# Deferring two groups' output projection until all weights are decoded, with one matmul type and a new issue order

## The chip, the cores and the metric

One core of a Trainium2 chip runs the whole program. The metric is the device time of one execution in microseconds (us), lower is better.

## The reference

Attention over 4 batches, 8 heads, 768 positions and 64 channels per head. Each query sees the keys within 15 positions of its own, and 24 block keys (the maximum over each block of 32 keys) whose values are block means; the softmax runs over both sets. The result, laid out as 3072 tokens of 512 values, goes through a gated feed-forward layer:

```python
rms = sqrt(mean(x * x) + 1e-6);  xn = x / rms * rms_g
g   = xn @ w_gate                    # 512 x 1536
h   = g * sigmoid(g) * (xn @ w_val)  # 512 x 1536
out = h @ w_out                      # 1536 x 512
```

The three weight matrices arrive as float64, two 32-bit words per value.

## The kernel before

**Units and groups.** The 3072 tokens are 24 units of 128. Units 0 to 5 (batch 0) have attention steps of their own in float32, `su_...`; units 6 to 23 have `load_unit`, `prep_k`, `scores`, `expo`, `attend`. `norm_a` and `norm_b` turn a unit's result into `xT`, the transposed f16 pair (high and low part) that the feed-forward layer reads. The feed-forward work goes by nine groups of 384, 128, 256 and then six times 384 tokens (`GROUPS`). The width 1536 of the hidden layer is 12 blocks f of 128.

**Feed-forward steps.** `gate_val g f T` makes two products of 12 f16 matmuls each into two PSUM banks (tile `gv`), then on ScalarE a tanh, on VectorE two multiplications, and splits the gated value `th` into a pair (`hh`, `hl`). `project g f` multiplies the pair with block f of w_out: for each 128 tokens a triple of 128x512 matmuls (hh with both parts of w_out, hl with one), summed over all f in a bank `acc`. Groups 5 to 8 make half or all of their gated values in another way (`make_s`, `make_t`, `seven`, `swish`); the change does not touch their arithmetic.

**Weights.** `load_gv n` (n from 0 to 11; even gate, odd value) and `load_o f` (f = 0, 2, ... 10) fetch 1 MB each. `decode` turns float64 into float32: one ScalarE and two VectorE instructions of 128x1024. `decode_gv` adds a ScalarE square; `split_gv` has nine small matmuls for a norm, a scale, one ScalarE and one VectorE instruction that leave the f16 pair in `w_gv`. `decode_o` leaves w_out first as a pair of float32r tiles (a ScalarE cast, a VectorE subtraction). Groups 0, 1 and 2 (`grp < HALF`) are projected with these float32r pairs, block by block while weights still arrive. Later `scale_h`, `row_o` (squares of w_out's rows) and `scale_o` give scales, and `conv_o` turns each float32r pair into an f16 pair: two GpSimd additions, two ScalarE and two VectorE instructions of 128x512 per pair of blocks. Groups from 3 on are projected with f16 pairs and these scales.

**Rooms.** Raw weights 0, 1 and 5 to 11 go through two buffers `raw`; 2, 3 and 4 through the rooms `wo0` to `wo2`; w_out's raw words through the room of their own block pair, `wo0` to `wo5`.

**Order.** `PLAN` is the list of steps in program order. `ORDER` then fixes, for each engine's queue separately, the exact order in which its instructions issue. Each queue is served in order, so an instruction that waits holds all that stand behind it. The DMAs that the SP queue issues follow its list as well. `WARM` puts extra matmuls into TensorE's queue in the first stage.

Of the kernel before, what the change touches and what calls it, by code (L numbers as in the profile page):

```python
# [19 lines left out]
P = 128  # L20
NEG = -1.0e30
EXPO = float(1 << 23)
HALF = 3
SEVEN = 5
RAW = 2
# [7 lines left out]
SR = 6  # L33
# [11 lines left out]
su_first; su_load 0 1; su_load 1 1; su_load 2 1; su_load 3 1; su_load 4 1; su_load 5 1; su_load 0 0;  # L45
load_gv 0 1; su_k 0; su_k 1; su_k 2; su_k 3; su_k 4; su_k 5; su_v 0; su_q 0; su_v 1; su_v 2; su_v 3; su_v 4;
su_v 5; su_load 1 0; load_gv 1 1; su_load 2 0; su_fill 0; decode_gv 0; su_scores 0 0; su_fill 2; su_q 1;
su_scores 0 1; su_vsum 0; su_q 2; su_expo 0 0; su_fill 1; su_vsum 1; su_fill 5; su_v2 0; load_gain;
su_expo 0 1; su_v2 2; su_scores 1 1; su_fill 3; su_vsum 4; prep_gain; su_scores 1 0; su_vsum 3; su_vsum 2;
load_gv 2 1; load_gv 5; su_vsum 5; split_gv 0; su_attend 0 0; su_v2 1; su_attend 0 1; su_expo 1 1; su_expo 1 0;  # L50
decode_gv 1; su_attend 1 0; su_attend 1 1; su_scores 2 0; su_fill 4; su_expo 2 0; norm_a 0; decode_gv 2;
load_gv 4 1; su_attend 2 0; load_gv 3 1; split_gv 2; split_gv 1; decode_gv 3; su_scores 2 1; load_o 0 1;
su_expo 2 1; norm_b 0; su_attend 2 1; split_gv 3; load_o 2 1; norm_a 2; decode_o 2; decode_o 0; norm_a 1;
decode_gv 4; norm_b 2; norm_b 1; su_v2 3; load_o 4 1; swap_left; gate_val 0 0 384; sum_load 1 0 0 0;
sum_load 1 0 0 1; split_gv 4; su_load 3 0; su_v2 4; sum_load 1 0 0 2; gate_val 0 1 384; decode_o 4;
decode_gv 5; su_q 3; sum_fold 1 0 0 0; split_gv 5; su_scores 3 0; sum_load 1 0 0 3; sum_fold 1 0 0 1;
project 0 0 384 0; su_expo 3 0; su_scores 3 1; su_expo 3 1; su_attend 3 0; sum_load 1 0 1 0; su_v2 5;
load_gv 6; su_attend 3 1; sum_load 1 0 1 1; decode_gv 6; norm_a 3; gate_val 0 2 384; load_gv 7; decode_gv 7;
sum_fold 1 0 0 2; load_o 6; norm_b 3; gate_val 0 3 384; sum_fold 1 0 0 3; split_gv 6; load_gv 8;
sum_fold 1 0 1 0; load_o 8; su_load 4 0; split_gv 7; load_o 10; sum_fold 1 0 1 1; sum_load 1 0 1 2;  # L60
project 0 1 384 0; sum_fold 1 0 1 2; load_gv 9; sum_load 1 0 1 3; sum_load 1 1 0 0; sum_load 1 1 0 1; su_q 4;
project 0 2 384 0; decode_o 6; su_scores 4 0; su_expo 4 0; sum_fold 1 0 1 3; sum_load 1 1 0 2; su_scores 4 1;
gate_val 0 4 384; sum_fold 1 1 0 0; project 0 3 384 0; su_expo 4 1; su_attend 4 0; sum_load 1 1 0 3;
su_load 5 0; su_attend 4 1; norm_a 4; sum_fold 1 1 0 1; sum_load 1 1 1 0; sum_scale 1 0; decode_gv 8;
project 0 4 384 0; sum_load 1 1 1 1; decode_o 8; sum_fold 1 1 0 2; decode_gv 9; gate_val 0 5 384; norm_b 4;
sum_fold 1 1 0 3; split_gv 8; project 0 5 384 0; load_gv 10; sum_fold 1 1 1 0; sum_load 1 1 1 2; su_q 5;
split_gv 9; load_ks 1; su_scores 5 0; su_expo 5 0; load_k 6; su_scores 5 1; su_expo 5 1; sum_load 1 1 1 3;
# [79 lines left out]
project 8 2 384 2688; project 8 3 384 2688; seven 8 3; swish 8 2 1; swish 8 2 0; project 8 4 384 2688;  # L147
project 8 5 384 2688; seven 8 4; swish 8 3 1; swish 8 3 0; seven 8 5; swish 8 4 1; project 8 6 384 2688;
swish 8 4 0; project 8 7 384 2688; swish 8 5 1; project 8 8 384 2688; swish 8 5 0; project 8 9 384 2688;
project 8 10 384 2688; project 8 11 384 2688  # L150
"""


# [1112 lines left out]
```

## Time and profile before

| | |
|---|---|
| median of 3 runs | 724.93 us (724.47 to 725.55) |
| span of the profiled execution, first to last instruction | 722.0 us |
| busy share of the span: TensorE / VectorE / ScalarE / GpSimd | 95% / 79% / 69% / 33% |
| mean granted TensorE clock, share of full speed | 0.990 |

The profile has one execution and its span; the timed runs also hold what lies before the first and after the last instruction, 724.9 - 722.0 = 2.9 us. PE is TensorE's matmuls, PEld its weight loads, DVE VectorE, ACT ScalarE, POOL GpSimd, SP the queue that issues most DMAs. A row that names line L378 or L373 or L375 is that of a helper (subtraction, cast, copy).

### The profile page before, as it was taken

The page shows a single profiled execution, that of the slowest core. Times are in us where ns is not written, and L with a number is a line of the kernel's source. Part 1 is how long each engine was busy: PE and PEld are TensorE (multiplying, and loading weights), DVE is VectorE, ACT ScalarE, POOL GpSimd, SP SyncE. Part 2 cuts the span into 40 slices and gives each one's busy share as a digit, 9 for nine tenths or more (in the row PEclk, how much of TensorE's full clock was granted, in tenths as well). Part 3 has the DMA queues.
Part 4 walks back from the last instruction along what each step waited for, and adds up shares of the span by engine and source line. Part 5 has one row for each costly group of instructions (what it writes and reads, how often), then busy time and mean ns, then how long its engine had stood idle before and what let it go on. Part 6 is the DMA issues. An engine that isn't in the chain of part 4 may idle for free.

```text
span 722.0 us, 16185 instructions
## 1 busy us (share of the span) xinstructions
PE 683.7 (95%) x5846; PEld 496.5 (69%) x5846; DVE 573.3 (79%) x1611; ACT 501.3 (69%) x1095; POOL 241.9 (33%) x333
## 2 busy tenths in 40 slices
PE   7985999998999999999999999998999999999997
PEld 4674677766777866565555555775888787878884
DVE  4599988889779887768999979999768976766443
ACT  2588676878678875677687868868769777744433
POOL 6451221634434644633143343623124302310000
PEclk9997999999999999999999999999999999999999
DMA  9988624545897786959458696586356543321001
GB/s 195 310 294 270 207 82 119 113 105 113 132 166 153 141 140 156 180 120 179 111 103 162 143 187 139 103 148 119 85 101 116 103 113 65 67 39 44 2 1 44
DMA packets 243861, 93.34 MB, mean 129 GB/s; under 512 B 227716, under 2 KB 227716, under 8 KB 243780
## 3 DMA queue, kind: packets, MB, share of 16 engines
q1 hardware_dynamic: 239172, 84.78, 55.6%
q10 hardware_dynamic: 3456, 6.29, 2.5%
q0 software_dynamic: 1152, 1.22, 0.9%
q8 instruction: 46, 0.75, 0.4%
q14 instruction: 35, 0.29, 0.1%
HBM read 50.45 MB, written 6.59 MB: 79 GB/s over the span
## 4 chain that ended last, share of the span: by engine, by line
PE 49%; DVE 16%; ACT 14%; DMA 10%; issue 6%; SPq 3%; POOL 2%; ACTq 0%; DVEq 0%; POOLq 0%
PE acc L1215 14%; PE gv L1185 14%; PE gv L1121 13%; ACT sm L799 3%; DMA eT<-ee 2%; PE att L956 2%; DMA hn<-in_v_dram 2%; DVE sm L788 1%; PE att L825 1%; DMA hn<-in_k_dram 1%; PE att L784 1%; DVE w L482 1%; SPq L695 1%; ACT junk L1015 1%; DMA qT<-qs 1%
## 5 line engine op out<-in xcount | busy, mean ns | idle before, releaser
L1185 PE MATMUL gv<-xT,w_gv 128*128 128x384 f16 (+2 forms) x1584 | 229.5, 298 | 7.8 <-DVE th L1190 5.2
L1185 PEld LDWEIGHTS <-w_gv 128*128 128x128 f16 x1584 | 141.0, 98 | 86.5 <-issue 19.0
L1215 PE MATMUL acc<-wo,hh 128*128 128x512 f16 (+1 forms) x576 | 178.7, 392 | 0.1
L378 POOL TENSOR_TENSOR ee<-sm,ee 128x256 f16<-128x256 f32 (+1 forms) x72 | 70.5, 995 | 132.6 <-ACT ee L373 107.1
L1215 PE MATMUL acc<-wo,hl 128*128 128x512 f16 (+1 forms) x288 | 110.8, 385 | 1.6 <-DVE hl L1173 1.5
L1121 PEld LDWEIGHTS <-w_gv 128*128 128x128 f16 x1008 | 84.2, 98 | 6.0 <-issue 1.5
L799 ACT ACTIVATE sm<-sm,mx,c 128x192 f32<-128x192 f32 x144 | 70.6, 538 | 2.8
L1215 PEld LDWEIGHTS <-hh 128*128 128x128 f16 x432 | 40.4, 98 | 31.2 <-ACT hh L373 0.5
L788 DVE CUSTOM_DVE_ANT_0 sm<-att,mask 128x192 f32<-128x192 f32 x144 | 45.6, 349 | 6.3 <-PE att L784 4.3
L1121 PEld LDWEIGHTS <-wo 128*128 128x128 f16 x540 | 44.8, 98 | 6.5 <-issue 4.0
L1121 PE MATMUL gv<-S,w_gv 128*128 128x192 f16 x504 | 48.4, 246 | 0.4 <-ACT R L1148 0.2
L1121 PE MATMUL gv<-xT,w_gv 128*128 128x192 f16 x504 | 47.0, 246 | 0.1
L373 ACT CAST hh<-th 128x384 f16<-128x384 f32 (+3 forms) x66 | 29.5, 446 | 23.7 <-DVE th L1192 12.3
L766 POOL DMA_DIRECT2D v2h<-v2h x36 | 19.7, 548 | 66.8 <-ACT v2h L765 62.0
L1189 ACT ACTIVATE th<-gv,gains 128x384 f32<-128x384 f32 (+2 forms) x66 | 33.9, 513 | 11.8 <-PE gv L1185 10.2
L1215 PEld LDWEIGHTS <-hl 128*128 128x128 f16 x216 | 21.1, 98 | 30.2 <-DVE hl L1173 3.9
L378 DVE TENSOR_TENSOR hl<-th,hh 128x384 f16<-128x384 f32 (+3 forms) x66 | 36.9, 563 | 6.1 <-ACT hh L373 5.8
L1170 DVE SCALAR_TENSOR_TENSOR att<-att,R 128x384 f32<-128x384 f32 x42 | 23.2, 562 | 21.1 <-ACT att L1169 20.8
L1190 DVE SCALAR_TENSOR_TENSOR th<-th,gv 128x384 f32<-128x384 f32 (+2 forms) x66 | 31.2, 473 | 10.0 <-ACT th L1189 9.7
L626 ACT ACTIVATE junk<-hn 96x512 uint8<-96x512 f32 x48 | 30.0, 625 | 12.3 <-DMA hn<-in_v_dram 8.9
L373 ACT CAST ee<-sm 128x256 f16<-128x256 f32 (+1 forms) x72 | 34.7, 507 | 2.2 <-DMA eT<-ee 1.6
L1121 PE MATMUL gv<-xT,wo 128*128 128x192 f16 x360 | 34.9, 246 | 1.2 <-ACT xT L1108 0.6
(276 smaller groups left out, 1485.7 us busy)
## 6 DMA issues: line engine op xcount, KB each, us to landing
wo<-in_moe_w_out_dram SPq DMA_DIRECT2D x6, 1024.0 KB
out_dram<-ob ACTq DMA_DIRECT2D x23, 256.0 KB
raw<-in_moe_w_val_dram SPq DMA_DIRECT2D x5, 1024.0 KB
hn<-in_k_dram SPq DMA_DIRECT2D x24, 192.0 KB
hn<-in_v_dram SPq DMA_DIRECT2D x24, 192.0 KB
qr_l<-in_q_dram SPq DMA_DIRECT2D x17, 256.0 KB
vr_l<-in_v_dram SPq DMA_DIRECT2D x17, 256.0 KB
raw<-in_moe_w_gate_dram SPq DMA_DIRECT2D x4, 1024.0 KB
```

The source lines that it names most:

```text
L373: nc.scalar.copy(o, i)
L378: (nc.vector if ENG.get(op, "p") == "v" else nc.gpsimd).tensor_tensor(o, a, b, op=ALU.subtract)
L626: nc.scalar.activation(junk[0:96], y[:, o:o + DM], AF.Square, accum_out=d["ss"][:, j:j + 1])
L766: {"s": nc.sync, "a": nc.scalar, "p": nc.gpsimd}[ENG.get("v2q", "a")].dma_start(v2h[other, r], v2h[rs, r])
L788: nc.vector.tensor_tensor_reduce(sm[:, i, :], pt[:, j * SC:(j + 1) * SC], mask, 1.0, NEG, op0=ALU.add, op1=ALU.max, accum_out=mx[:, i:i + 1])
L799: nc.scalar.activation(sm[:, i, :], sm[:, i, :], AF.Exp, scale=s["c"][:, 0:1], bias=mx[:, i:i + 1])
L1121: nc.tensor.matmul(bank[:, i * T2:(i + 1) * T2], lhsT=right(n, wi, c), rhs=left(xi, c), start=start, stop=(i == 1 and c == 1 and wi == 1), ...
L1170: nc.vector.scalar_tensor_tensor(th, th, 1.0, g, op0=ALU.add, op1=ALU.mult)
L1185: nc.tensor.matmul(pt[:, 0:T], lhsT=w_gv[:, f - f % 2 + i, wi, c, f % 2, :], rhs=x[:, xi, c, 0:T], start=(n == 0), stop=(n == 3 * NC - 1))
L1189: nc.scalar.activation(th[:, 0:T], pg[:, 0:T], AF.Tanh, scale=f_sc[:, f - f % 2:f - f % 2 + 1])
L1190: nc.vector.scalar_tensor_tensor(th[:, 0:T], th[:, 0:T], 1.0, pg[:, 0:T], op0=ALU.add, op1=ALU.mult)
L1215: nc.tensor.matmul(accs[grp][j], lhsT=h[:, js], rhs=wo_hl[f // 2][:, wi, f % 2, :], start=(f == first and n == 0), stop=(f == (first - 1) ...
```

## The change

Group 2 is projected with f16 pairs from the start (`HALF` is gone; `KEEP = 2`). Groups 0 and 1 are gated as before, but their gated values stay in float32 in SBUF (`kept`, tiles `h0` and `h1`); when w_out has been scaled, `halve` makes the f16 pair just before each `project`. No float32r pair of w_out exists any more: `decode_o` writes float32 words in place, `conv_o` scales from them without the GpSimd additions. Raw gate and value weights take turns in the six `wo` rooms (`ROOMS`), and w_out is loaded behind them, so load n + 6 waits for decode n. The output copies of groups 0 to 2 go from VectorE to ScalarE. Some buffers of units 2 to 7 lie elsewhere (`kr_e`, `vv`, `h1`, `hhl`), and `set_v` fills the constant columns of `vv` after batch 0 instead of at the start. `PLAN` has all gate and value decodes ahead of w_out's, group 0's gates without projections between them, then group 1's, and then `project 0 ...` and `project 1 ...`; `ORDER` is new for every queue. `WARM` is unchanged.

```diff
-HALF = 3
+KEEP = 2
+ROOMS = (0, 1, 2, 3, 5, 4)
...
         def load_gv(n):
             f, i = n - n % 2, n % 2
-            shape = [P, NC, 4 * P]
-            raw = wo_room(n - 2, shape, U32) if 2 <= n < 5 else pools["early"].tile(shape, U32, name="raw", bufs=RAW)
+            raw = wo_room(ROOMS[n % 6], [P, NC, 4 * P], U32)
...
         def decode_o(f):
-            w = decode(raws.pop(("o", f)))
-            wo_hl[f // 2] = wo_room(f // 2, [P, 2, 2, DM], F32R)
-            hi, lo = (wo_hl[f // 2][:, j].rearrange("p f d -> p (f d)") for j in range(2))
-            copy("wo", hi, w)
-            sub("wolo", lo, w, hi.bitcast(F32))
+            decode(raws.pop(("o", f)), wo_raw[f // 2][:, 0:2 * DM])
...
         def conv_o(i):
-            w = wo_hl[i]
-            t = []
-            for a in range(2):
-                x = pools["late"].tile([P, DM], F32, name="cv", bufs=4)
-                nc.gpsimd.tensor_tensor(x, w[:, 0, a].bitcast(F32), w[:, 1, a].bitcast(F32), op=ALU.add)
-                t.append(x)
...
+            w = wo_raw[i][:, 0:2 * DM].bitcast(F32).rearrange("p (a x) -> p a x", a=2)
+            n = wo_hl[i] = wo_raw[i][:, 2 * DM:4 * DM].bitcast(F16).rearrange("p (j a x) -> p j a x", j=2, a=2)
             for a in range(2):
                 sc = hs_t["o_sc"][:, 2 * i + a:2 * i + a + 1]
-                nc.scalar.activation(n[:, 0, a], t[a], AF.Copy, scale=sc)
+                nc.scalar.activation(n[:, 0, a], w[:, a], AF.Copy, scale=sc)
...
         def gate_val(grp, f, T):
+            if grp < KEEP:
+                if grp not in kept:
+                    kept[grp] = pools["early"].tile([P, NF, T], F32, name=f"h{grp}")
+                th = kept[grp][:, f]
             else:
-                hh = mp.tile([P, 384], F32R, name="hh")
-                hl = mp.tile([P, 384], F32R, name="hl")
+                th = mp.tile([P, 384], F32, name="th")[:, 0:T]
...
+            if grp >= KEEP:
+                hh, hl = hs[grp, f] = half_pair()[1:]
+                copy("hh", hh[:, 0:T], th)
+                sub("hl", hl[:, 0:T], th, hh[:, 0:T])
+
+        def halve(grp, f, T):
+            hh, hl = hs[grp, f] = half_pair()[1:]
+            th, sc = kept[grp][:, f], hs_t["h_sc"][:, 0, f:f + 1]
+            nc.scalar.activation(hh[:, 0:T], th, AF.Copy, scale=sc)
+            nc.vector.scalar_tensor_tensor(hl[:, 0:T], th, sc, hh[:, 0:T], op0=ALU.mult, op1=ALU.subtract)
...
         def project(grp, f, T, tok0):
+            if grp < KEEP:
+                halve(grp, f, T)
...
-                    if grp < HALF:
-                        copy("ob", ob, accs[grp][j].rearrange("p (h d) -> p h d", h=H))
-                    else:
-                        nc.scalar.activation(ob, accs[grp][j].rearrange("p (h d) -> p h d", h=H), AF.Copy, scale=hs_t["o_iv"])
+                    nc.scalar.activation(ob, accs[grp][j].rearrange("p (h d) -> p h d", h=H), AF.Copy, scale=hs_t["o_iv"])
```

## Rows read from the trace of the kernel before

**Rows 1.** Busy time per stretch: PE, PEld, DVE, ACT, POOL, granted clock, DMA share, GB/s

```profile
40.00:80.00 40.00, 30.00 (x221) 22.71 (x221) 38.47 (x88) 31.86 (x48) 13.70 (x20) 0.87 0.76 245
80.00:160.00 80.00, 78.48 (x573) 57.79 (x571) 69.25 (x174) 56.84 (x109) 26.37 (x34) 1.00 0.45 120
200.00:260.00 60.00, 55.99 (x523) 46.40 (x520) 50.45 (x154) 48.40 (x114) 29.08 (x32) 1.00 0.86 156
...
340.00:500.00 160.00, 155.84 (x1255) 100.11 (x1252) 148.15 (x421) 122.85 (x283) 60.01 (x67) 1.00 0.68 134
...
72.28:260.20 187.92, 178.73 (x1477) 137.11 (x1477) 162.66 (x463) 140.14 (x312) 76.07 (x89) 0.99 0.63 134
```

**Rows 2.** PE in order of time: the first gates, and group 3's first

```profile
64.75 0.50 PE L1185 MATMUL gv<-xT,w_gv 128*128 128x384 f16 x1
...
72.88 2.11 PE L1185 MATMUL gv<-xT,w_gv 128*128 128x384 f16 x12 [1.43 <-DVE th L1190]
...
260.16 4.07 PE L1185 MATMUL gv<-xT,w_gv 128*128 128x384 f16 x24 [1.23 <-DMA xT<-xs]
```

**Rows 3.** VectorE in order of time, before and at the first gated value

```profile
65.34 1.22 DVE L378 TENSOR_TENSOR wo<-w,wo 128x1024 fp32r<-128x1024 f32 x1
...
67.67 1.22 DVE L378 TENSOR_TENSOR wo<-w,wo 128x1024 fp32r<-128x1024 f32 x1
68.80 1.28 DVE L481 TENSOR_SCALAR w<-w 128x1024 uint32<-128x1024 uint32 x2
70.01 1.22 DVE L482 SCALAR_TENSOR_TENSOR w<-wo,w 128x1024 uint32<-128x1024 uint32 x1
...
72.28 0.54 DVE L1190 SCALAR_TENSOR_TENSOR th<-th,gv 128x384 f32<-128x384 f32 x1
```

**Rows 4.** PE in order of time: projections in float32r, then one in f16

```profile
111.58 2.12 PE L1185 MATMUL gv<-xT,w_gv 128*128 128x384 f16 x12
113.41 0.75 PE L1215 MATMUL acc<-wo,hh 128*128 128x512 f32 x2
...
114.24 0.62 PE L1215 MATMUL acc<-wo,hh 128*128 128x512 f32 x2
...
114.93 0.63 PE L1215 MATMUL acc<-wo,hh 128*128 128x512 f32 x2
...
344.77 2.76 PE L1185 MATMUL gv<-xT,w_gv 128*128 128x384 f16 x16
347.37 0.59 PE L1215 MATMUL acc<-wo,hh 128*128 128x512 f16 x2
...
348.02 0.60 PE L1215 MATMUL acc<-wo,hh 128*128 128x512 f16 x2
```

**Rows 5.** One line's instructions: min/median/max ns, first and last start in us

```profile
L1215 PEld LDWEIGHTS <-hh x432: 96/98/181, 273.1 to 717.4; 128*128 128x128 f16 x144
...
L1215 PEld LDWEIGHTS acc<-wo,hh x144: 186/190/333, 82.2 to 266.7; 128*128 128x128 f32 x144
...
L530 DVE SCALAR_TENSOR_TENSOR w_gv<-w,w_s,w_gv x12: 1271/1276/2123, 42.0 to 159.5; 128x1024 f16<-128x1024 f32 x12
```

**Rows 6.** Groups of instructions: count, busy us, mean ns, idle before and releaser

```profile
L378 DVE TENSOR_TENSOR wo<-w,wo 128x1024 fp32r<-128x1024 f32 x6 | 8.2, 1368 | 0.6 <-ACT wo L373 0.6
...
L375 DVE COPY ob<-acc 128x512 f32<-128x512 f32 x6 | 4.0, 678 | 0.0
...
L601 DVE SCALAR_TENSOR_TENSOR wo<-cv,scales,wo 128x512 f16<-128x512 f32 x12 | 10.0, 838 | 0.0
...
L593 POOL TENSOR_TENSOR cv<-wo 128x512 f32<-128x512 f32 x12 | 17.1, 1435 | 11.6 <-DVE wo L601 9.6 <-ACT junk L626 1.2 <-ACT th L1189 0.8
...
L439 POOL MEMSET v2l<- 128x528 f16 x1 | 0.5, 537 | 0.0
```

**Rows 7.** Waits of the SP queue: us in total, times, longest

```profile
SPq L500 <- DVE w L482: 23.2, 3, 9.2
...
SPq L494 <- DVE w L482: 15.9, 4, 7.2
```

More of the change, by code (lines that the diff above doesn't have):

```diff
@@ L50 @@
[L50 to L64, printed above, removed]
@@ L332, in close_pool, with raw_rows @@
             del pools[name]
-        def raw_rows(name, shape):
+        def raw_rows(name, shape, u=0):
             if "late" in pools:
                 return pools["late"].tile(shape, F32, name=f"{name}_l", bufs=LB)
+            if u % 2 and name != "v2r":
+                return pools["early"].tile(shape, F32, name=f"{name}_e")
             return pools["ap"].tile(shape, F32, name=name)
@@ L472, in prep_gain, with decode @@
                 nc.vector.tensor_scalar(ivg[:, j:j + 1], i, 0.5 + 0.5 * j, None, op0=ALU.mult)
-        def decode(raw):
+        def decode(raw, out=None):
             hi, lo = raw[:, :, 1], raw[:, :, 0]
@@ L832, in attend @@
                                                den.broadcast_to([P, 4, D]), op0=ALU.mult, op1=ALU.mult)
+        groups = GROUPS
         k32 = {}
@@ L847, in su_load @@
                 x = su[0, t] = pools["ap"].tile([P, H, D], F32, name="vr" if t % 2 else "kr")
+                load_rows(x, src[0, :, t * P:(t + 1) * P, :])
+                return
+            if which == 0 and t == 2:
+                x = su[0, t] = pools["early"].tile([P, H, D], F32, name="kr_e")
                 load_rows(x, src[0, :, t * P:(t + 1) * P, :])
@@ L868, in su_room, with half_pair @@
                 return pools["start"].tile([P, n], F32, name=name, bufs=SU)
-            o = {"k32": 0, "v1f": 768, "v2f": 1296}[name]
-            return w_gv[:, SR + 2 * (t - SU):SR + 2 * (t - SU) + 2].rearrange("p n j c a x -> p (n j c a x)").bitcast(F32)[:, o:o + n]
+            if t == SU:
+                o = {"k32": 0, "v1f": 768, "v2f": 1296}[name]
+                return w_gv[:, NF - 2:NF].rearrange("p n j c a x -> p (n j c a x)").bitcast(F32)[:, o:o + n]
+            if name == "k32":
+                if 1 not in kept:
+                    kept[1] = pools["early"].tile([P, NF, groups[1]], F32, name="h1")
+                return kept[1][:, NF // 2 * (t - SU - 1):NF // 2 * (t - SU)].rearrange("p f x -> p (f x)")
+            if t == SU + 1:
+                return half_pair()[0][:, 0:1536].bitcast(F32)[:, 0:n]
+            o = {"v1f": 0, "v2f": 528}[name]
+            return vv.rearrange("p j x -> p (j x)").bitcast(F32)[:, o:o + n]
+        kept = {}
+        def half_pair():
+            t = mp.tile([P, 1536], F16, name="hhl")
+            return t, t[:, 0:768], t[:, 768:1536]
         def su_tile(shape, name, other, bufs):
@@ L1162, in swish @@
             if (grp, f2) not in h_of:
-                h_of[grp, f2] = [mp.tile([P, 768], F16, name=n) for n in ("hh", "hl")]
+                h_of[grp, f2] = half_pair()[1:]
             f = 2 * f2 + a
@@ L1208, in project @@
             if f == first:
-                accs[grp] = [att["pool"].tile([P, 512], F32, name="acc1") if grp == 1 else
-                             ps.tile([P, 512], F32, name="acc", bufs=3) for _ in range(T // P)]
+                accs[grp] = [ps.tile([P, 512], F32, name="acc", bufs=3) for _ in range(T // P)]
+            if grp < KEEP:
+                halve(grp, f, T)
             hh, hl = hs.pop((grp, f))
```

529 lines of the change are left out of this document (293 added, 236 removed).

## The prediction

> **What bounds the kernel now.** I read the busy time by stretch first, then TensorE's order of time around the projections, then VectorE's before the first gated value. From 72.28 us, the first gated value on VectorE, to 260.2 us, the start of group 3, TensorE is busy 178.7 of 187.9 us, VectorE 162.7, ScalarE 140.1, GpSimd 76.1 [rows 1]. TensorE sets the pace there, and VectorE stands close behind at 87%. In 40 to 80 us it is the other way round: VectorE is busy 38.5 of 40 us while TensorE has 30.0, some of it `WARM` matmuls, at a mean granted clock of 0.87 [rows 1]. The reader is to see in that pair that the first stage ends when VectorE has done its list, and that what comes behind it ends when TensorE has. The rows of VectorE show what the end of its first stage is made of: decodes of w_out and their subtractions, up to the first `th` at 72.28 [rows 3], while the next gate on TensorE waits 1.43 us for VectorE [rows 2]. The first gate itself starts at 64.75.
>
> So two things can shorten the time: less VectorE work ahead of the first gated value, and less TensorE work behind it. Everything else in the change counts only if it makes one of these two wait.
>
> **Part 1: the projections of groups 0, 1 and 2 in f16.** 216 matmuls with float32r operands (144 with hh, 72 with hl) become f16. They come as 72 triples. An f16 triple takes 348.02 - 347.37 = 0.65 us. A float32r triple behind another takes 114.93 - 114.24 = 0.69, so 0.04 more. One that follows matmuls of another line takes 114.24 - 113.41 = 0.83; but the 12 matmuls in front of it then stand 113.41 - 111.58 = 1.83 us, where 16 such matmuls in front of an f16 triple stand 2.60 us, or 1.95 for 12 [rows 4]. The first float32r matmul only starts 0.12 early, so the net price is 0.83 - 0.65 - 0.12 = 0.06, and I take 0.07. The longer weight load is the reason in the rows: 190 ns against 98 ns [rows 5]. Read entry by entry, the written issue list of before has 49 triples behind another line and 23 behind a triple. The saving is 49 x 0.07 + 23 x 0.04 = 4.4 us. The bounds are 72 x 0.04 = 2.9 and 72 x 0.18 = 13.0 (0.83 against 0.65, nothing given back). I take 4.4, because a start that moves forward and a next start that does not is no loss.
>
> A page of the Trainium skill, TensorE: Matmul & The Clock Gate, says in Step-by-step: what each phase is for that the next tile's weights load while this tile's matmul runs, and in Back-to-back issue gap that a gap is set by the columns, about 216 ns for 512 of them in an isolated stream. The f16 rows agree (0.65 / 3 = 0.217 us), the float32r rows differ by the 0.04 to 0.07 us above; by the page alone this part would bring 0 and the sum would be 4.4 us higher.
>
> **Part 2: what stands before the first gated value.** In the written list of VectorE before, three `decode_o` (f = 2, 0, 4, two instructions each) and two float32r subtractions stand ahead of the first `th`. In the changed list there are none of these, but one `decode_gv` more (seven, not six). A decode is 0.64 + 1.22 = 1.86 us, a subtraction 1.22 [rows 3]. Removed: 3 x 1.86 + 2 x 1.22 = 8.0; added 1.86; net 6.1 us. VectorE is 96% busy in 40 to 80 us [rows 1], so nearly all of it should move the start. Against it: TensorE's changed list puts the matmuls of `split_gv 6` ahead of the first gate, so the start waits for ScalarE's square of weight 6, which waits for its load and decode. Bounds 0 and 6.1; I take 5.
>
> **Part 3: VectorE and ScalarE in the stretch behind it.** The same window of 162.7 us VectorE loses four subtractions (4 x 1.37 = 5.5) and the four output copies that lay in it (4 x 0.68 = 2.7) [rows 6]. It gains the three `decode_o` that moved behind the first gate (5.6, less 1.9 for the `decode_gv` that moved ahead), and two `conv_o` that ran after it before (4 x 0.84 = 3.4) [rows 3, 6]. `halve` costs what the subtraction and cast of the two groups cost, one instruction for one. That leaves 161.6 us in a stretch that part 1 shortens to 187.9 - 4.4 = 183.5: VectorE would have to be busy 88%, against 87% now. TensorE's work is no longer mixed with the decodes: the 144 projection matmuls of groups 0 and 1 stand behind the last decode of w_out, so the front of the stretch is denser for VectorE than the back, and a projection cannot start before `scale_o` and `conv_o`, which need all six w_out blocks. What VectorE can be filled to is in rows: 96% in 40 to 80 us, 93% in 340 to 500, 87% in 80 to 160, 84% in 200 to 260 [rows 1]. At 93% nothing is lost. At 87% (162.7 / 187.9) the stretch takes 161.6 / 0.866 = 186.6, a loss of 3.1; at 84% it takes 192.4, a loss of 8.9. I take 2 us, near the middle of the first two, for the wait of the first projection behind `scale_o`.
>
> **Parts costed at nothing.** GpSimd's twelve additions (17.1 us) go [rows 6]; at 76.1 of 187.9 us busy it holds nobody for long, and if it did the gain is at most the idle time named below. `set_v` moves five small instructions of it to the end of batch 0, covered by the same idle time; without the cover the next unit's values would come at most 5 x 0.54 = 2.7 us later, if all five cost what the largest does [rows 6]. ScalarE loses six casts and gains six output copies and is 75% busy in the stretch [rows 1]. The weight loads: in the SP queue, L494 and L500 already wait 15.9 and 23.2 us for decodes [rows 7]. The changed list keeps such waits (load n + 6 behind decode n, w_out behind decodes 6 to 11), and the loads of units 3 to 5 and the block sums stand behind them. Six rooms instead of two plus the next ones make each wait earlier in the need, so I take 0; the price if not is in the slower rival.
>
> **The sum.** 722.0 - 4.4 - 5 + 2 = 714.6 us of span; with the 2.9 us that the runs hold around it, 717.5. Group 3's first gate should start at about 260.2 - 7.4 = 253 us.
>
> **Rivals.** A difference under about 0.2% (1.5 us) cannot be told from no change here: faster means below 723.5, slower above 726.4.
>
> *The long load is hidden anyway.* TensorE would have filled those 0.04 to 0.07 us with waits that it has in any case. For it: 9.2 us of the stretch hold no matmul at all [rows 1]. Against it: inside runs of triples no wait is listed and the pitch is still 0.69. Then 722.0 - 5 + 2 + 2.9 = 721.9. The page named above would give this too.
>
> *Nothing gained.* The first gate starts no earlier because of `split_gv 6` in front of it, and VectorE costs 3 to 4 us more: 722.0 - 4.4 + 4 + 2.9 = 724.5. For it: TensorE's queue is strictly in order. Against it: VectorE, the busiest engine there, has 6.1 us less to do.
>
> *VectorE becomes the bound (slower).* With no projections between gates, TensorE asks for a new pair of weights every two gates (48 matmuls at 0.1625 [rows 4], 7.8 us), and VectorE must decode and split two weights for it (2 x 1.86 + 2 x 1.28 = 6.3 us [rows 3, 5]) beside the gates and units 3 to 5. TensorE then starves in front and has 144 projections left behind. It decides where VectorE's share of the stretch falls below 161.6 / (187.9 + 5) = 83.8%, 5 us being the lead of part 2. At 82% the time is 722.0 + 197.1 - 187.9 - 5 + 2.9 = 729; at 80% it is 734. For it: 84% in 200 to 260 us. Against it: that stretch had waits on transfers, and 96% stands in the stretch that is most like this one [rows 1].
>
> *More than forecast.* The waits of the stretch go with the old order: with half of the 9.2 us without matmuls gone and no loss in part 3, 717.5 - 2 - 4.6 = 711; with part 1 at its upper bound too, 702.
>
> **How the numbers follow.** Forecast (711 to 721): 0.50. Load hidden (721 to 723.5): 0.15. More than forecast (below 711): 0.13. Nothing gained: 0.07. Slower: 0.15. So faster 0.78, same 0.07, slower 0.15. The time is that of the likeliest case, 717.5. The range runs from 705, which leaves out the last part of the fourth rival, to 728, which takes in the near part of the slower one and leaves out its far part, together no more than 2 in 10.
>
> **What would show it.** No `acc` matmul or weight load in f32; triples of 0.65 us in groups 0 to 2; the first `th` of group 0 on VectorE at about 67 us, not 72.28; the last `w_gv` subtraction well before 159.5 us, where it is now [rows 5], at about 115; no `cv` additions on GpSimd; group 3's first gate near 253. Wrong would be: waits of gates for `w_gv` splits between 80 and 120 us, waits of the first projections for `conv_o` or `hl` of more than 5 us, a granted clock below 1.0 there, or a first gate no earlier than 64.75.

## The result and the profile after

The changed kernel takes 715.18 us, median of 4 runs (713.28 to 716.97); the kernel before took 724.70 beside it (4 runs, 723.89 to 725.55). The ratio is 0.9878, 95% interval 0.9852 to 0.9903: faster by 1.2%, and 2.3 us below the forecast of 717.5. The profiled execution of the changed kernel is its fastest: 713.28 us with a span of 711.4, while its other three had spans of 712.6 to 715.1. Among the executions reported below, one of E7's ten (2455.59 us) and one of the kernel before beside E9 to E11 (880.89 us) were slow ones; they count in the medians and in no ratio.

The windows of the changed kernel, columns as in [rows 1]; the third runs from the first gated value to group 3's first gate, the last from there to the end:

```profile
80.00:120.00 40.00, 40.00 (x308) 28.45 (x307) 36.81 (x99) 28.27 (x51) 11.26 (x16) 1.00 0.39 120
80.00:160.00 80.00, 69.04 (x659) 52.82 (x658) 67.13 (x175) 54.80 (x113) 30.47 (x40) 1.00 0.45 117
66.47:253.75 187.28, 173.95 (x1457) 120.84 (x1456) 157.24 (x461) 144.79 (x318) 62.37 (x83) 0.98 0.60 137
253.75:711.40 457.65, 446.62 (x3972) 317.71 (x3972) 343.25 (x980) 308.43 (x707) 125.98 (x157) 1.00 0.57 109
```

The last stretch of the kernel before, for which no row stands ahead of the prediction:

```profile
260.16:722.00 461.84, 447.48 (x3968) 316.44 (x3968) 357.96 (x992) 315.58 (x711) 133.21 (x155) 1.00 0.52 106
```

TensorE of the changed kernel in order of time: the first gate, a run of f16 projections, group 3's first gate.

```profile
62.20 0.48 PE L1251 MATMUL gv<-xT,w_gv 128*128 128x384 f16 x1
...
179.63 4.48 PE L1285 MATMUL acc<-wo,hhl 128*128 128x512 f16 x20
183.94 0.38 PE L1251 MATMUL gv<-xT,w_gv 128*128 128x256 f16 x2
...
253.75 1.46 PE L1251 MATMUL gv<-xT,w_gv 128*128 128x384 f16 x8 [0.51 <-DVE S L1148]
```

VectorE of the changed kernel, its first gated value:

```profile
66.47 0.56 DVE L1261 SCALAR_TENSOR_TENSOR h<-h,gv 128x384 f32<-128x384 f32 x1 [1.14 <-ACT h L1260]
```

One line's instructions of the changed kernel: the weight loads of all projections (first and last start: 169.9 and 707.1), and the splits of the gate and value weights.

```profile
L1285 PEld LDWEIGHTS <-hhl x864: 95/98/101, 169.9 to 707.1; 128*128 128x128 f16 x173
...
L587 DVE SCALAR_TENSOR_TENSOR w_gv<-w,w_s,w_gv x12: 1254/1278/2250, 36.2 to 116.0; 128x1024 f16<-128x1024 f32 x12
```

The reader is to see where the 10.6 us between the two spans (722.0 and 711.4) lie. The first gated value comes 72.28 - 66.47 = 5.8 us earlier. The stretch from it to group 3 is 187.28 us long, where it was 187.92 [rows 1]: 0.6 gained. The stretch behind group 3's first gate is 461.84 - 457.65 = 4.2 shorter. So the lead is there, the stretch in which TensorE's work was cut brings almost nothing, and a stretch costed at nothing brings more than a third.

Inside the middle stretch a hole has opened. TensorE was busy 78.48 of 80 us in 80 to 160 [rows 1] and is busy 69.04 now; the loss lies in its second half, since from 80 to 120 us it is busy 40.00 of 40.00. Windows of the changed kernel in it:

```profile
125.00:170.00 45.00, 33.79 (x397) 29.50 (x395) 31.91 (x99) 29.95 (x76) 17.84 (x23) 0.92 0.53 121
145.00:160.00 15.00, 6.61 (x97) 5.80 (x97) 10.08 (x20) 10.34 (x28) 7.95 (x13) 0.97 0.46 102
160.00:166.30 6.30, 6.17 (x43) 5.16 (x43) 2.95 (x15) 4.84 (x15) 0.00 (x0) 0.52 0.44 109
```

TensorE of the changed kernel in order of time, at two gates of group 1:

```profile
146.82 1.45 PE L1251 MATMUL gv<-xT,w_gv 128*128 128x128 f16 x23 [2.76 <-DVE h L1263]
...
160.13 6.30 PE L1251 MATMUL gv<-xT,w_gv 128*128 128x128 f16 x42 [4.07 <-DVE h L1261]
...
166.41 3.71 PE L1251 MATMUL gv<-xT,w_gv 128*128 128x256 f16 x30
```

The row at 160.13 merges two shapes. Its groups, kept apart by form:

```profile
L1251 PE MATMUL gv<-xT,w_gv 128*128 128x256 f16 x18 | 3.8, 402 | 0.0
L1251 PE MATMUL gv<-xT,w_gv 128*128 128x128 f16 x24 | 2.7, 312 | 4.1 <-DVE h L1261 4.1
```

Its waits between 125 and 170 us (in total, times, longest):

```profile
PE gv L1251 <- DVE h L1261: 6.9, 6, 4.1
...
PE gv L1251 <- DVE h L1263: 4.2, 6, 2.8
```

And its chain of work that ended last, at the longest of these waits:

```profile
154.25 0.73 ACT junk L673 x2
...
155.01 0.73 ACT junk L624 x2
...
158.78 0.72 ACT junk L624 x2
```

Group 1's gates are short (24 matmuls of 128 columns, about 1.5 us) and have only the two `gv` banks; each waits until VectorE has read a bank. At 160.13 the reason lies in ScalarE's list: a square of `hn` (L673) that waits for a load, and then six of the twelve row squares of w_out (`junk L624`, some 0.75 us each with the reading of their sums, from 155.01 to 159.50), stand ahead of the tanh that group 1's gate needs. Then the granted clock is at its lower level, 1.2 GHz (0.52), for 6.3 us: 24 matmuls of 128 columns and 18 of 256 take 6.30 us. At the pace of the rows at 146.82 (1.45 / 23 = 0.063 each) and 166.41 (3.71 / 30 = 0.124) they would take 24 x 0.063 + 18 x 0.124 = 3.7, so the lower clock costs TensorE some 2.6 us there, by this estimate.

### The profile page after: what moved, and what is told of

It is laid out like the page before. It is cut to its first block, busy times and chain, and to the rows that moved or that the text cites. A ratio compares the mean times of both kernels' runs of the same rounds, so it can differ in the third digit from the quotient of the medians.

```text
span 711.4 us, 16135 instructions
## 1 busy us (share of the span) xinstructions
PE 676.8 (95%) x5846; PEld 481.3 (68%) x5846; DVE 548.1 (77%) x1599; ACT 495.7 (70%) x1095; POOL 221.4 (31%) x321
## 4 chain that ended last, share of the span: by engine, by line
PE 62%; DMA 10%; DVE 10%; ACT 8%; issue 4%; SPq 4%; POOL 1%; ACTq 0%; DVEq 0%; POOLq 0%
PE gv L1251 19%; PE gv L1187 16%; PE acc L1285 16%; DMA eT<-ee 4%; SPq L742 3%; PE att L831 2%; PE att L872 2%; DMA qT<-qs 2%; ACT sm L846 1%; PE att L1023 1%; DMA hn<-in_k_dram 1%; DMA hn<-in_v_dram 1%; DVE sm L835 1%; ACT ee L428 1%; DMA v2r_l<-in_v_dram 1%
## 5 line engine op out<-in xcount | busy, mean ns | idle before, releaser
L1251 PE MATMUL gv<-xT,w_gv 128*128 128x384 f16 (+2 forms) x1584 | 248.0, 300 | 12.9 <-DVE h L1261 6.9
L1285 PE MATMUL acc<-wo,hhl 128*128 128x512 f16 x864 | 229.8, 379 | 1.1 <-ACT hhl L1238 0.7
L1285 PEld LDWEIGHTS <-hhl 128*128 128x128 f16 x864 | 81.6, 98 | 66.9 <-DVE hhl L1273 3.0
L831 PE MATMUL att<-kT,qT 128*128 128x192 f16 x288 | 41.1, 246 | 4.1 <-DMA qT<-qs 2.2
L872 PE MATMUL att<-vv,eT 128*128 128x65 f16 x720 | 41.7, 193 | 1.3 <-DMA eT<-ee 1.2
L872 PEld LDWEIGHTS <-eT 128*128 128x128 f16 x720 | 34.2, 97 | 12.8 <-issue 2.0
L1260 ACT ACTIVATE th<-gv,gains 128x384 f32<-128x384 f32 (+1 forms) x42 | 22.8, 543 | 23.7 <-PE gv L1251 23.3
L433 POOL TENSOR_TENSOR xs<-x,xs 128x512 f16<-128x512 f32 x21 | 26.5, 1263 | 40.0 <-ACT xs L428 40.0
L1261 DVE SCALAR_TENSOR_TENSOR th<-th,gv 128x384 f32<-128x384 f32 (+1 forms) x42 | 21.5, 512 | 20.7 <-ACT th L1260 20.6
L679 POOL TENSOR_TENSOR hn<-hn 96x512 f32<-96x512 f32 x18 | 24.1, 1339 | 40.2 <-DMA hn<-in_v_dram 23.6
L673 ACT ACTIVATE junk<-hn 96x512 uint8<-96x512 f32 x48 | 30.0, 624 | 8.1 <-DMA hn<-in_v_dram 4.9
```

The lines of the kernel that those rows point to most:

```text
L433: (nc.vector if ENG.get(op, "p") == "v" else nc.gpsimd).tensor_tensor(o, a, b, op=ALU.subtract)
L673: nc.scalar.activation(junk[0:96], y[:, o:o + DM], AF.Square, accum_out=d["ss"][:, j:j + 1])
L679: eng.tensor_tensor(x[:, 0:w], x[:, 0:w], y[:, 0:w], op=op)
L831: nc.tensor.matmul(pt[:, j * SC:(j + 1) * SC], lhsT=s["qT"][:, a * H + h, :], rhs=kT[:, h, :], start=(a == 0), stop=(a == 1))
L872: nc.tensor.matmul(po[r][:, h // 2, 0:D + 1], lhsT=e, rhs=vv[:, 0:D + 1], start=(n == 0), stop=(n == len(pairs) - 1))
L1251: nc.tensor.matmul(pt[:, 0:T], lhsT=w_gv[:, f - f % 2 + i, wi, c, f % 2, :], rhs=x[:, xi, c, 0:T], start=(n == 0), stop=(n == 3 * NC - 1))
```

## The experiments

Twelve kernels ran, in four sets; each set shares its runs of the kernel before (medians 723.05, 723.05, 724.00 and 722.75 us over 17 to 23 runs). "th" is the first gated value on VectorE, "g3" group 3's first gate, "tail" from g3 to the end of the span. The lists in `ORDER` are long rows of numbers; a move in them is written as a line taken out and put in by the names of steps.

**E1, f16 pairs alone, in the kernel before.** No lists are touched. Left out: the scale that would bring hh and w_out into the range of f16.

```diff
         def decode_o(f):
-            wo_hl[f // 2] = wo_room(f // 2, [P, 2, 2, DM], F32R)
+            wo_hl[f // 2] = wo_room(f // 2, [P, 2, 2, 2 * DM], F16)[:, :, :, 0:DM]
...
-                hh = mp.tile([P, 384], F32R, name="hh")
+                hh = mp.tile([P, 768], F16, name="hh")
```

> The kernel before, with one thing changed: hh, hl and the pairs of w_out that groups 0, 1 and 2 read are f16 tiles instead of float32r. The scale that the changed kernel uses is left out here, so the f16 pairs hold unscaled values. The lists of issue, the instruction counts and the places in SBUF stay. Theory of the prediction (the f16 weight load is shorter, a triple shrinks from 0.69 or 0.83 us to 0.65): 4.4 us off the time before, so 720.3 us, bounds 2.9 and 13. First gate of group 3 about 4 us earlier than 260.2. Rival (the weight load is hidden behind matmuls anyway): the triples keep their pitch, 724.7 us, no change.

Measured: 723.12 us (12 runs, 718.75 to 724.77), ratio 0.9997 [0.9983, 1.0011]. Its window from th to g3, and its weight loads:

```profile
73.41:261.51 188.10, 175.99 (x1476) 122.56 (x1476) 161.67 (x463) 140.06 (x312) 75.61 (x89) 0.98 0.65 134
```

```profile
L1216 PEld LDWEIGHTS <-hh x576: 95/98/181, 83.3 to 716.9; 128*128 128x128 f16 x192
```

Two triples of E1 in one row, where before they stood 0.69 us apart [rows 4]:

```profile
114.41 0.59 PE L1216 MATMUL acc<-wo,hh 128*128 128x512 f16 x2
...
115.06 0.59 PE L1216 MATMUL acc<-wo,hh 128*128 128x512 f16 x2
```

The loads fell from 190 to 98 ns, the triples to 115.06 - 114.41 = 0.65 us, and TensorE's busy time in the stretch from 178.73 [rows 1] to 175.99. The stretch is 188.10 us, not shorter than 187.92. What TensorE saved, it stands idle.

**E2, more banks for group 1, in the changed kernel.** Every second gate of group 1 uses the three `acc` banks, which are free until the first projection.

```diff
-            pg = ps.tile([P, 512], F32, name="gv", bufs=2)
+            bank, n_banks = ("acc", 3) if grp == 1 and f % 2 else ("gv", 2)
+            pg = ps.tile([P, 512], F32, name=bank, bufs=n_banks)
```

> The changed kernel, with the odd gates of group 1 writing their two products into the three banks named acc, which stand idle until the first projection, instead of the two banks named gv. Nothing else changes, the lists of issue stay. In the trace after, the stretch from 125 us to the first projection at 169.96 us is about 17 us longer than TensorE's own work in it. Theory A (banks: with two banks the next gate of group 1 must wait until tanh and both VectorE products of the one before are done): the waits of TensorE for L1261 and L1263 in 125 to 160 us, some 9.5 us in all, nearly vanish, the first projection starts 8 to 12 us earlier, and the time falls from 715.2 to about 705. Theory B (ScalarE's list: the sums of squares of w_out stand in a row ahead of the last two tanhs and of the scale that every pair of w_out needs): the squares stay where they are in the list, behind transfers of hn, the first projection moves by under 3 us, and the time stays within 712 to 715. Theory C (VectorE has no time, as the prediction had it): no change.

**E3, row squares earlier, in the changed kernel.** ScalarE's list, and the place where the squares' unused result goes (a free half of the w_out room).

```diff
 ScalarE's list, groups 0 and 1
-    row_o 0 ... row_o 5: twelve squares, between the last tanhs of group 1
+    the first eight one by one behind earlier tanhs of group 1, from the second on
```

> The changed kernel with another order on ScalarE alone: the twelve sums of squares of w_out are taken out of their row behind the tanh of gate 1 9 and put one by one behind the tanhs of gates 1 1 to 1 11, each once its block is decoded; the tanhs of gates 1 10 and 1 11 so stand ahead of the last four. Their thrown-away product goes to the half of the w_out tile that is free then, instead of the tile junk. Theory B (the list): the wait of 4.07 us before 160.13 shrinks to under 1, the slow clock behind it goes with it, the first projection starts at 163 to 166 instead of 169.96 us, and the time falls by 4 to 6 us to about 710. Theory A (banks alone): the gates stay at about 2.6 us each; the squares between them make the round trip longer, and the first projection starts no earlier than 168; time 714 to 717. Theory C (VectorE): no change.

**E4, both, and one w_out decode earlier.** E2 and E3 together, with `decode_o 8` farther forward in VectorE's list.

> The changed kernel with the banks of the second experiment, the squares of the third (those of the last blocks now behind the tanhs of gates 1 9 and 1 11), and the last decode of w_out (decode_o 8) moved forward in VectorE's list, from behind gate 1 9 to behind gate 1 3. If the 17 us are two holds on one path (A and B), neither alone gives all and both give most of it: first projection at 154 to 158 us, time about 702 to 705. If the gain of an earlier first projection is given back later (waits for attention or for transfers of units 6 to 11), first projection early but the first gate of group 3 not before 250 and the time no lower than 712. If C is right (VectorE), no change.

Measured: E2 715.74 us (6 runs), 0.9910 [0.9879, 0.9940]; E3 714.80 (6), 0.9889 [0.9866, 0.9912]; E4 712.79 (5), 0.9856 [0.9831, 0.9880]. TensorE's waits between 125 and 170 us, those of group 1's gates (`gv`) among them, in E2, then E3, then E4:

```profile
PE gv L1252 <- DVE h L1262: 3.7, 2, 2.1
PE att L634 <- DVE tmp L632: 2.6, 1, 2.6
PE att L1043 <- ACT ee L1036: 2.2, 2, 1.9
PE att L696 <- ACT junk L673: 1.6, 1, 1.6
PE gv L1252 <- DVE h L1264: 1.6, 2, 1.3
```

```profile
PE gv L1251 <- DVE h L1263: 3.7, 6, 2.4
PE gv L1251 <- DVE h L1261: 2.8, 6, 0.7
```

```profile
PE att L1043 <- ACT ee L1036: 2.3, 2, 1.4
PE att L696 <- ACT junk L673: 2.1, 1, 2.1
PE gv L1252 <- DVE h L1262: 1.7, 1, 1.7
PE gv L1252 <- DVE h L1264: 1.6, 2, 1.4
```

The 11.1 us of the gates' waits fall to 5.3, 6.5 and 3.3, but other waits come up in E2 and E4: with them 11.7 and 8.2 us are listed (one of 0.5 in E4 and two in E3 are not shown, which make E3's total 7.5). So E2 moved the waits, and E3 and E4 took a third and a quarter of them away. The first projection, at 169.96 in the changed kernel, starts at 172.11, 169.37 and 166.51; the 8 to 12 us, the 4 to 7 us and the 12 to 16 us that the three expectations hoped for did not come. TensorE is busy 36.71 of the 45 us in E4, not 33.79. The time hardly follows: by the ratios E3 and E4 lie inside the changed kernel's interval (0.9852 to 0.9903), and E2 lies above it, with an interval that overlaps. E4 has the lowest median of the versions that are not short of work; that it beats the changed kernel is not shown.

**E5 and E6, less TensorE work.** The projections of groups 0 to 2, all but the first matmul of each sum, go over 256 of 512 columns, in the kernel before (E5) and in the changed one (E6); half of these outputs is left out.

```diff
-                    nc.tensor.matmul(accs[grp][j], lhsT=h[:, js], rhs=wo_hl[f // 2][:, wi, f % 2, :],
+                    N = DM if grp > 2 or f == first and n == 0 else DM // 2
+                    nc.tensor.matmul(accs[grp][j][:, 0:N], lhsT=h[:, js], rhs=wo_hl[f // 2][:, wi, f % 2, 0:N],
```

> The kernel before, with the projections of groups 0, 1 and 2 on 256 of their 512 columns (all but the first matmul of each sum; the other half of those outputs is left out). Counts and lists of issue stay. This takes some 20 us of work from TensorE ahead of the first gate of group 3 and nothing from any other engine. If TensorE sets the pace between the first gated value and group 3, as the prediction read it: first gate of group 3 near 242 instead of 260.16 us, time 703 to 707. If the chain through ScalarE's and VectorE's lists and the transfers they stand behind sets it (the theory after the f16 experiment, which gave TensorE 8 us and the time nothing): first gate of group 3 not before 256, time 719 to 724.

> The changed kernel with the same cut: projections of groups 0 to 2 on 256 of 512 columns. It takes some 22 us of work from TensorE, nearly all between 170 and 254 us, where it is busy 82 of 84 us. If TensorE sets the pace there: first gate of group 3 near 235 to 240 instead of 253.75 us, time 697 to 702. If the attention of units 6 to 8 behind the sums of batch 1 sets it here too (the last transpose into xT of group 3 is issued 5 to 6 us ahead of group 3's first gate in every run so far): first gate of group 3 not before 249, time 710 to 715.

Measured: E5 723.52 us (10 runs), 0.9989 [0.9967, 1.0012]; E6 712.60 (4), 0.9840 [0.9804, 0.9877]. Windows from th to g3, E5 and then E6:

```profile
72.15:255.20 183.05, 161.44 (x1476) 131.50 (x1476) 158.48 (x453) 140.24 (x312) 77.47 (x88) 0.98 0.64 136
```

```profile
67.29:254.36 187.07, 161.92 (x1458) 123.41 (x1456) 156.97 (x460) 144.16 (x316) 62.91 (x83) 0.95 0.58 134
```

TensorE has 178.73 - 161.44 = 17.3 us less work in E5's stretch, and the kernel before gains at most 0.33%, 2.4 us. (E5's profiled execution is its fastest, 719.11 us, 4.4 below its median; its 183.05 is not the usual length.) In E6 TensorE has 12.0 us less; the stretch is as long as before (187.07), and the median 2.6 us lower, with an interval that overlaps the changed kernel's. So TensorE's projection work does not set the pace in the kernel before, nor behind 170 us in the changed one, where E6's cut lies. What TensorE waits for longest in the kernel before is VectorE's first product of a gate, behind the tanh; these waits from 72 us to group 3, before and in E5:

```profile
PE gv L1185 <- DVE th L1190: 4.5, 3, 1.7
```

```profile
PE gv L1185 <- DVE th L1190: 13.2, 10, 3.5
```

(In E1 they are 8.0 us.) That the lists of VectorE and ScalarE set the pace there is therefore a live rival, and no run takes much work from either inside this stretch. The gates of the changed kernel are not tested either: from 80 to 120 us TensorE is busy without a pause.

**E7 and E9, less decoding ahead of th, in the kernel before.** E7: VectorE's two decode instructions of w_out blocks 0, 2 and 4 on 64 of 1024 columns. E9: all their decode instructions on both engines, and their subtraction. These blocks' values are left out (in E9 their cast reads the gain vector).

```diff
+            m = 64 if f < 6 else 2 * DM
-            w = decode(raws.pop(("o", f)))
+            w = decode(raws.pop(("o", f)), m)
```

> The kernel before, with VectorE's two decode instructions of w_out blocks 0, 2 and 4 on 64 of 1024 columns (most of their decoding is left out; ScalarE's part, the subtractions and all counts and lists stay). VectorE loses about 5 us of work ahead of the first gated value and half a us behind it. If the lead is what carries the gain of the change (part 2 of the prediction): first gated value near 67 to 68 instead of 72.28 us, first gate of group 3 by the same 4 to 5 us earlier, time 718 to 720. If what holds the stretch behind are transfers that keep their own time (loads of hn, the key and value sums of batch 1): the first gated value comes earlier, group 3 by under 2 us, time 722 to 725.

> The kernel before, with the decode of w_out blocks 0, 2 and 4 cut on both engines: ScalarE's Prelu, VectorE's two decode instructions and its subtraction work on 64 of 1024 columns, and the copy to float32r reads the gain vector, so that it waits for no decode (most of these blocks' values are left out; counts and lists stay). That takes some 8 us from VectorE and 3 us from ScalarE ahead of and around the first gated value, where the cut on VectorE alone brought that value only 1.5 us forward, since ScalarE's list held its tanh. Theory L (the gain of the change is the decode work it writes behind the first gates, on both engines, and this lead keeps to the end): first gated value at 66 to 68 instead of 72.28 us, time 717 to 719. Rival (what holds the stretch behind keeps its own time): the first gated value comes that much earlier, the first scores of unit 6 less than 2 us, and the time stays at 722 to 724.

Measured: E7 721.31 us (10 runs), 0.9968 [0.9949, 0.9988]; E9 722.02 (12), 0.9975 [0.9960, 0.9990]. The tanh of the first gated value on ScalarE in E7, then VectorE's th in E7 and in E9:

```profile
69.83 0.58 ACT L1191 ACTIVATE th<-gv,gains 128x384 f32<-128x384 f32 x1
```

```profile
70.79 0.55 DVE L1192 SCALAR_TENSOR_TENSOR th<-th,gv 128x384 f32<-128x384 f32 x1
```

```profile
70.08 0.55 DVE L1204 SCALAR_TENSOR_TENSOR th<-th,gv 128x384 f32<-128x384 f32 x1
```

Three decodes of 1.86 us, cut to six short instructions, are some 5 us of VectorE. They bring th only 1.5 us forward (72.28 to 70.79), and cutting ScalarE's part too brings 2.2: the tanh itself comes late, at 69.83, and th cannot start ahead of it. In the changed kernel the same step comes at 66.47; the other 3.6 us come with what else it changes ahead of th, which no run took apart. The ratios are worth 2.3 and 1.8 us, about as much as th moved, but in these two traces group 3's first gate comes at 260.09 and 259.22, only 0.1 and 0.9 us earlier than the 260.16 of the kernel before.

**E8, three more moves in E4's lists.**

```diff
 VectorE:  gate 1 6's second product ahead of the rest of unit 5's norm
 TensorE, VectorE: `sum_scale 1 1` behind the sums of the row squares
 ScalarE:  the last two squares of hn behind the tanhs of gates 1 10 and 1 11
```

> The fourth experiment, with four more places in the lists changed: on VectorE the second product of gate 1 6 goes ahead of the norm of unit 5, and the scale of the value sums goes behind the first half of the scale of w_out; on TensorE the matmul of that scale of the value sums, which waits for transfers of hn, goes from ahead of gate 1 11 to just ahead of the scale of w_out; on ScalarE the squares of the last two hn pieces go behind the tanhs of gates 1 10 and 1 11. If the hole of 125 to 170 us is made by places in in-order lists behind transfers of hn, TensorE now runs the gates of group 1 with under 3 us of waits, the first projection starts at 160 to 164 (166.5 in the fourth experiment, 169.96 after the change) and the time is 706 to 710. If transfers of unit 6 come late instead (queries and keys of the first attention behind the hole), the first projection moves but group 3 does not, and the time stays at 711 to 714.

Measured: 713.79 us (6 runs), 0.9871 [0.9837, 0.9906]. The first projection starts at 170.57, not at 160 to 164. The largest part of the waits comes back in one place, the first gate of group 2 (waits of TensorE, 125 to 170 us):

```profile
PE gv L1252 <- DMA xT<-xs: 5.0, 1, 5.0
```

**E10, a later start, in the changed kernel.** Nine ScalarE copies ahead of the first tanh, into a tile not yet in use.

```diff
+            if (grp, f) == (0, 0):
+                for _ in range(9):
+                    nc.scalar.copy(kept[0][:, NF - 1], gb[:, 0:T])
```

> The changed kernel, with nine copies of the gain vector (some 0.5 us each, 4.7 us in all) in ScalarE's list right ahead of the first tanh; nothing else. Theory L (a shift of the first gated value is a shift of all that follows): first gated value near 71 instead of 66.47 us, first projection, first scores of unit 6 and first gate of group 3 later by 4 to 5 us, time 719 to 720. Rival (there is slack between the first gates and the queries of unit 6): under 1.5 us of it reach group 3's first gate, time 715 to 717.

Measured: 717.42 us (6 runs), 0.9911 [0.9890, 0.9932]. VectorE's th and TensorE's g3 in E10:

```profile
69.26 0.56 DVE L1264 SCALAR_TENSOR_TENSOR h<-h,gv 128x384 f32<-128x384 f32 x1 [3.94 <-ACT h L1263]
```

```profile
258.57 3.73 PE L1251 MATMUL gv<-xT,w_gv 128*128 128x384 f16 x22 [0.24 <-DVE S L1148]
```

th comes 2.8 us later, g3 4.8 later than in the changed kernel's trace, and the median is 2.2 us higher. In this trace a start that is late stays late. The time alone does not show it, since the two intervals overlap, and the profiled execution (719.12 us) is 1.7 above its median.

**E11, unit 6 earlier, in E4's lists.** Does the attention of the next batch set the pace behind the hole?

```diff
 VectorE, ScalarE: prep of unit 6's queries and its first four scores, some steps forward
 TensorE: the scores' matmuls likewise
```

> The fourth experiment, and on top of it the queries of unit 6 earlier in the lists: their load goes ahead of the transpose for unit 4 on the queue of SyncE, their square, scale, split and transpose go among the gates 1 9 to 1 11 (the square's thrown-away product goes to a free half of a w_out tile), and the first scores of unit 6 with what follows them on VectorE and ScalarE go ahead of the first projections. In all ten traces so far the first gate of group 3 comes 76.7 to 79.0 us after the first scores of unit 6, however much work TensorE has between. Theory Q (the attention of units 6 to 8, started by the queries of unit 6, sets group 3's first gate, and that the end): first scores of unit 6 at 160 to 166 us instead of 172.45, first gate of group 3 at 238 to 246 instead of 249.25, time 704 to 709. Rival (TensorE sets it after all, or the keys and values of units 7 and 8 do): first scores earlier, group 3's first gate not before 248, time 711 to 714.

Measured: 714.77 us (6 runs), 0.9886 [0.9859, 0.9912]. TensorE in E11, unit 6's first scores and g3:

```profile
169.76 0.82 PE L831 MATMUL att<-kT,qT 128*128 128x192 f16 x8
...
254.23 3.74 PE L1252 MATMUL gv<-xT,w_gv 128*128 128x384 f16 x22
```

In ten traces, from both kernels, g3 had come 76.7 to 79.0 us behind these scores (78.1 to 79.9 in those of E9, E10 and E12). Here it comes 254.23 - 169.76 = 84.5 behind: the scores moved, g3 did not. So group 3's first gate does not simply follow these scores. The test is a weak one: the scores were meant to start at 160 to 166 and came only 2.7 us ahead of E4's 172.45.

**E12, two waits of the tail taken away, in the kernel before.** TensorE's two longest waits for VectorE behind group 3 are 1.5 us each and have no counterpart in the changed kernel. Before, from 260.16 us on:

```profile
PE att L825 <- DVE mx L788: 1.5, 1, 1.5
PE acc L1215 <- DVE hl L1173: 1.5, 1, 1.5
...
PE gv L1121 <- ACT xT L1108: 0.6, 2, 0.3
```

```diff
 VectorE's list only
     two score instructions of unit 16, three places forward
     one subtraction `hl` of group 5, some places forward
```

> The kernel before, with three entries of VectorE's list moved, all behind the first gate of group 3: the first two maxima of the scores of unit 16 go three places forward, and the last subtraction of one swish of group 5 goes five places forward. In the four traces of the old lists TensorE waits for these entries 1.5 us each (436 to 439 and 499 to 501 us in the trace of before: L788 and L1173); in the traces of the new lists there is no such wait. The stretch from group 3's first gate to the end is 460.0 to 462.1 us long in the traces of the old lists and 457.7 to 460.6 in those of the new ones. Theory W (behind group 3 TensorE sets the pace, and what the new lists gain there is such waits): the two waits shrink to under 0.4 us each, that stretch shortens by 2 to 3 us, and the time falls to 720 to 722 (ratio 0.996 to 0.998). Rival (the wait moves to the next transfer or to the next list entry): the two waits go, others grow, the time stays (ratio 0.999 to 1.001).

Measured: 724.15 us (12 runs), 1.0016 [0.9999, 1.0033]. The same waits in E12's trace:

```profile
PE gv L1121 <- ACT xT L1108: 1.9, 2, 1.6
...
PE acc L1215 <- DVE hl L378: 0.8, 1, 0.8
```

Both waits are gone, others have taken their place, and nothing is gained.

## Why the prediction came out right, and which step failed

**Part 1 failed (f16, -4.4).** The step is "TensorE sets the pace there", which turned a shorter triple into time. The arithmetic of triples holds: the f16 ones stand at (183.94 - 179.63) / 20 = 0.2155 us a matmul, 0.65 a triple, and the loads at 98 ns. But E1 has all of it and gains 0.03%, and 17.3 us less TensorE work gains no more than 0.33% (E5). The rival "the long load is hidden anyway", to which I gave 0.15, names what happened, time that TensorE stands idle in any case; the load itself was not hidden, since the triples did get shorter. What misled was the busy share: 95% in the stretch says how often a matmul is in flight, not what the next one waits for. The better view was there before the change. The kernel before's chain by line in 72 to 254 us:

```profile
by line: PE gv L1185 18.1%; PE acc L1215 10.6%; DMA eT<-ee 7.5%; DMA hn<-in_v_dram 6.6%; issue 6.4%; PE att L956 3.6%; DMA hn<-in_k_dram 2.5%; DVE v2l L767 2.1%; DVE th L1192 2.1%; DVE w L482 1.9%; ACT junk L571 1.9%; PE att L995 1.8%; POOL
```

Gates and projections hold 29% of that chain; the rest are loads, the matmuls of attention, and small VectorE and ScalarE work, in series. It is no proof by itself: the projections' 10.6% are 19 us, and E5 cut 17.3 us of TensorE's work there for next to nothing. The Trainium skill, Perfetto Trace Analysis, Identifying the Most-Contended Engine, says that matmul busy time is no good measure of how near TensorE is to its roofline, and names the weight loads' busy share as one of two to use instead. Here that is 137.11 / 187.92 = 73%, below VectorE's 87% [rows 1]; E5 agrees that the 95% mislead. Whether VectorE is the one is not tested: E7 and E9 take their work from it ahead of the stretch, not inside it.

**Part 2 held in size (-5).** Among kernels whose lists up to g3 and whose work behind th are untouched, th is at 72.28, 73.41 and 72.03 with the old lists (before, E1, E12; mean 72.57) and at 66.47 and 67.17 with the new ones (after, E2; mean 66.82): 5.75 us. g3 follows at 260.16, 261.51 and 259.17 against 253.75 and 255.73, means 260.28 and 254.74, 5.5 us. (E1 has other operand types and E2 other banks; E5 and E6, which lack work in the stretch, are left out.) So in these five traces the lead is nearly whole at group 3, and E10's trace shows the same in the other direction. Against it stand the traces of E7 and E9, where of 1.5 and 2.2 us ahead of th only 0.1 and 0.9 are left at g3, though their ratios (0.9968 and 0.9975) gain as much as th moved. That the lead carries the gain fits most of the record and is not shown beyond it. Its reason was too narrow: less decoding gives 1.5 to 2.2 us of the 5.75 (E7, E9).

**Part 3 named the wrong wait (+2).** Against 78.48 us busy in 80 to 160 [rows 1], TensorE is 9.4 less busy there, and it meets the clock's lower level. The first projection, whose wait behind `scale_o` the 2 us were for, has no wait listed before it; it is group 1's gates that wait, 11.1 us, for two banks and for tanhs behind the row squares. VectorE has 157.24 us of work in the stretch, not 161.6. Yet the stretch as a whole is 0.6 us shorter, so with part 1 at nothing the loss in it is nothing too. What the hole itself costs stays open: E3 and E4 take only a third and a quarter of its waits away, E2 and E8 mostly move them, and E4's first projection and g3, 3.5 and 4.5 us earlier than in the changed kernel's trace, come with a time whose interval overlaps.

**"Parts at nothing" missed the tail.** Behind g3 the spans of six traces with the old lists are 461.84, 459.99, 462.10, 461.01, 460.88 and 461.53 us (before, E1, E5, E7, E9, E12; mean 461.2), of eight with the new lists 457.65, 458.27, 460.63, 458.05, 457.94, 458.90, 458.73 and 458.17 (after, E2, E3, E4, E6, E8, E10, E11; mean 458.5): 2.7 us. TensorE's work there is the same (447.48 and 446.62 us busy); it stands 14.4 us in the one and 11.0 in the other. The other engines have less work there: VectorE 357.96 us before and 343.25 after, ScalarE 315.58 and 308.43, GpSimd 133.21 and 125.98. Part of it is `conv_o`, which behind g3 runs in the kernel before and not in the changed one (VectorE before, from 260.16 us on):

```profile
L601 DVE SCALAR_TENSOR_TENSOR wo<-cv,scales,wo 128x512 f16<-128x512 f32 x5 | 4.8, 959 | 0.0
```

Part 3 charged this move to the stretch ahead of g3, and the sum gave the tail nothing for it. The other steps in `PLAN` there differ by little, but `ORDER` was rewritten to the end, and I costed a rewritten list at nothing without reading it there. Which of the two brings the 2.7, the moved work or the order, stays open: the two longest of the old waits are not it (E12). Putting one kernel's lists behind group 3 into the other wasn't tried, since the buffers that the two lists hand on differ.

**The sum.** Predicted -4.4 - 5 + 2 + 0 = -7.4. Measured, by the means above: 0 (E1), -5.5 up to g3, -2.7 behind it, -8.2 together; the ratio makes it 724.7 x 0.0122 = -8.8. The total came out near by luck: a gain that is not there and a loss that the stretch does not show left -2.4, where a gain not foreseen brought -2.7. Of the 2.9 us that the sum adds to the span, 1.9 are the time outside it in one execution (713.28 and 711.4); the other 1.0 is how far the profiled execution of the kernel before lay below its median, by that figure.

**The signs.** No f32 projection, triples of 0.65, th at 66.47 for "about 67", the last split at 116.0 for "about 115", g3 at 253.75 for "near 253", the first gate at 62.20 against 64.75: all as written. Of the signs of a wrong forecast one came: a granted clock below 1.0 in the hole. Whether it costs time is not shown. What sets the pace between 170 and 254 us in the changed kernel is not settled: TensorE's projections are not it (E6), and moving unit 6's first scores did not move g3 (E11). Its chain there is more TensorE's than before (first line of the chain by line, 72 to 254 us, changed kernel):

```profile
by line: PE gv L1251 37.0%; PE acc L1285 11.5%; issue 4.6%; DMA qT<-qs 3.2%; DMA eT<-ee 3.1%; DMA hn<-in_v_dram 3.1%; PE att L1023 2.9%; ACT junk L624 2.4%; DVE wo L647 1.9%; PE att L1062 1.8%; PE att L1043 1.6%; SPq L742 1.6%; PE att L831 
```

## What to carry to other kernels

A stretch in which TensorE is 95% busy need not be bound by it: before costing a saving at its full size, read which lines the chain of work goes through, and take a large piece of the work away to see whether the stretch gets shorter. A lead of 5.75 us at the first gated value was still 5.5 us some 190 us later, in five traces; waits removed one by one inside the lists mostly reappeared one place farther on. And a prediction that hits its total should still be tested term by term: here three of four terms were wrong and their errors cancelled.

## What the runs showed of the hardware that was not expected

After a wait of 4.07 us, in a stretch where TensorE was busy 6.61 of 15 us, the granted clock stood at 0.52 (1.2 GHz) from 160.0 to 166.3 us while TensorE was busy 6.17 of these 6.30; 24 matmuls of 128 columns and 18 of 256 took 6.30 us. Executions of one kernel differ by several us without any change to it: E1's twelve runs go from 718.75 to 724.77, so one profiled span settles nothing below about 3 us, half of that spread. Several marks above (E4, E7, E9, E10, E11) stand on one trace each and are to be read with that in mind.
